# A fused attention and MLP kernel whose work is in one hand-held list: the first keys loaded one head at a time, and the list reordered

## The chip, the cores and the metric

The kernel runs on one core of a Trainium2 chip. A core has a matrix engine (TensorE, "PE"; its weight loads are shown apart as "PEld"), a vector engine (VectorE, "DVE"), an activation engine (ScalarE, "ACT"), a general engine (GpSimd, "POOL") and a queue engine (SyncE, "SP") that here only issues DMAs. Each engine runs its own instructions in program order and waits on semaphores for the others. Sixteen DMA engines serve all queues. The metric is the device time of one execution in microseconds (us), lower is better. A profiled execution gives a trace; its span is the time from the first to the last instruction, a little under the device time.

## What is computed

Causal attention over 4 batches, 8 heads, 768 tokens and 64 dimensions, then a two-layer MLP. Heads 0, 2 and 6 ("retrieval") see the whole past; the other five ("streaming") see the last 64 keys and the first 4.

```python
scores = scale * np.matmul(q, k.transpose(0, 1, 3, 2))
...
stream_keep = causal & (is_sink | in_win)
...
a = np.exp(scores)
a = a / (np.sum(a, axis=-1, keepdims=True) + 1e-09)
return np.matmul(a, v).astype(np.float32)
...
h = x @ w_in
g = np.maximum(h, 0.0) + alpha * np.minimum(h, 0.0)
return (g @ w_out).astype(np.float32)
```

x is the attention output with the heads side by side: 3,072 tokens of 512. w_in is 512 x 2048, w_out 2048 x 512, alpha one slope per hidden unit. All inputs are fp32 in DRAM; the kernel computes in bf16 and accumulates in fp32.

## The kernel before

**Pieces.** Two heads form a pair: (2,6), (1,5), (0,4), (3,7), four pairs in each batch, sixteen in all, numbered n = 0 to 15. A pair is a full 128 partitions: head hh = 0 in the lower 64, hh = 1 in the upper 64. The MLP works on token groups t = 0 to 7, two to a batch: 512 tokens (t even) and 256 (t odd).

**Items.** Every step is a named item, a small function that emits the instructions of one step:

- `Lq`n, `Lk`n, `Lv`n load a pair's fp32 queries, keys and values (lines 203 to 247), nearly all through SP's queue. For pair 0 the queries are two items, Lq0.0 and Lq0.1, and the keys one, Lk0, whose first head goes through ACT's queue and the second through SP's. `La` loads the slopes through ACT's queue. `wi`0 to 7 and `wo`0 to 3 load w_in and w_out in pieces through POOL's queue, with a cast. P items 0 to 3 need wi0 and wi1, 4 to 7 wi2 and wi3, 8 to 11 wi4 and wi5, 12 to 15 wi6 and wi7; the u-th quarter of an O item needs wo(u).
- `Cq`, `Ck`, `Cv` cast them to bf16, on POOL, ACT or DVE by a table (for n = 1 to 5 on POOL; Cq6 and Cq7 on ACT; later ones on DVE). `Tq`, `Tk` transpose on PE, `tq`, `tk` copy the result out of PSUM (tk on DVE for n under 4, on ACT for 4 to 7). From pair 8 on, `Dq` and `Dk` transpose by DMA from SP's queue instead.
- `S`n.hh.m is a part of the scores (PE), `s` its exponential (ACT), `m` its mask (DVE, from pair 4 on; before that the mask is added by PE, lines 462 and 501). `A`n.hh multiplies by the values (PE), `a` divides (DVE), `X`n transposes the pair's output into xT: by PE with the copy `x` for pairs 0 to 3 and 15, else by DMA from SP.
- `P`t.f is the first MLP layer for a block of 128 hidden units (two blocks for t odd); its three parts P0.f.0 to P0.f.2 take the pairs as they come. `p` is the negative half (ACT), `g` joins the halves (DVE). `O`t.s.u is a quarter of the second layer for 128 tokens, `o` copies it out of PSUM (ACT) and sends it to DRAM (POOL's queue for t under 6, else SP's). The last 128 tokens are done in three column cuts, `L0` to `L2` with `l0` to `l2`.
- `warm`0 to 8 are matmuls on zeros whose result nobody reads (32, 3, 14, and six times 4): they keep PE busy while it waits for the first loads. The rest (`kz`, `vz`, `sz`, `nms`, `nmr`, `id`, `near`, ...) fills constants and masks. A few items, such as m8.0.2, emit nothing.

**The order.** ORDER, a list of 1,076 names, is walked once; each engine and each DMA queue gets its instructions in that order. The list is the schedule: there is no other. The batches overlap by it: while the MLP of one batch runs on PE, the attention of the next one is woven in. Below, "pass one" is the stretch in which batch 0's MLP runs beside pairs 4 to 7, "pass two" batch 1's MLP beside pairs 8 to 11, "pass three" batch 2's beside 12 to 15.

**Bursts.** From pair 4 on, scores listed near each other are gathered and emitted as one burst. An item that can't stand beside them, such as a P, O or A item, ends the gathering. If each head of the burst has at least 576 columns, the two heads' matmuls are interleaved, each on half of PE's rows (line 430); if not, they run one by one on all rows, with zeros in the other half of the keys (line 423).

**PSUM.** Eight banks of PSUM are handed out by `take` (the one given back longest ago among the choices) and given back by `give`, both at the time of emission; the banks of the three cuts are not given back.

Of the kernel before, what the change touches and what calls it, by code (L numbers as in the profile page):

```python
# [14 lines left out]
busy zero La id warm0 kz3 Lq0.0 sz1 vz2 nms nmr so1 vz0 Lq0.1 Lk1 warm8 warm5 warm3 kz1 qz0 one Lq1 Lk0 Ck0.0 Cq0.0  # L15
Tq0.0 tq0.0 Tk0.0 qz kz0 kz2 idf warm2 Lk2 tk0.0 Ck1.0 Ck1.1 Cq0.1 Tk1 S0.0.1 s0.0.1 Tq0.1 S0.0.0 Cq1 warm7 Lv0 tk1.0
sz2 vz1 vz3 Tq1 Lq2 Ck0.1 S0.0.2 s0.0.0 tk1.1 Tk0.1 Ck2.1 tq1 S1.1.0 s0.0.2 Ck2.0 warm4 tq0.1 nz0 s1.1.0 Cq2 tk0.1 Cv0
Lk3 S0.1.0 kfz0 Lv1 vo ro0 Ck3.1 s0.1.0 Lq3 Ck3.0 wi1 wi0 Cq3 sz0 S1.0.0 so2 Al s1.0.0 so0 al S0.1.1 s0.1.1 Lv2 Tq2
Tk2 tk2.1 tk2.0 S0.1.2 S1.0.1 A0.0 s0.1.2 a0.0 Cv1 A0.1 a0.1 Cv2 s1.0.1 tq2 S1.1.1 nz1 Tk3 S2.0.1 tk3.0 s1.1.1 S2.0.2
X0 s2.0.1 x0 wi6 s2.0.2 wi7 Lv3 Lq5 Tq3 tk3.1 S2.0.0 wi5 m4.0.2 warm6 S2.1.0 A1.0 a1.0 Lk4 s2.0.0 A2.0 S2.1.1 A1.1  # L20
a2.0 tq3 s2.1.0 a1.1 S3.0.0 s2.1.1 s3.0.0 A2.1 a2.1 S3.1.1 X1 S3.0.1 s3.0.1 Lk5 wi4 kfz2 Cv3.0 Cq5 Lk7 wi2 X2 Ck4.0
s3.1.1 S3.1.0 x1 P0.0.0 x2 P0.0.1 A3.0 P0.1.0 P0.1.1 Lk6 Lq4 Lq6 Ck4.1 kfz3 nr Cv3.1 s3.1.0 A3.1 Lv7 Lv5 Lq7 Ck5.0 wi3
a3.0 P0.2.0 Tq5 tq5 P0.3.0 P0.3.1 a3.1 X3 x3 ns kfz1 P0.2.1 Tk4 near2 P1.2 P0.1.2 P0.2.2 P0.0.2 p1.2 p0.1 g0.1 Ck5.1
P1.0 P0.3.2 g1.2 P0.15 tk4.0 p0.2 g0.2 p0.15 wo0 p1.0 Lk8 near0 g0.15 g1.0 ro1 P1.12 P1.14 m12.1.2 p0.0 g0.0 wo1 tk4.1
p1.12 P0.14 g1.12 p0.14 g0.14 P0.13 p0.13 g0.13 P0.11 p1.14 Tk5 Ck7.1 g1.14 P1.10 tk5.0 p0.11 p1.10 Ck6.0 Ck7.0 g0.11
m8.0.2 tk5.1 wo2 Lv6 Lv4 P0.10 P0.8 p0.8 Tk7 g1.10 wo3 Cq4 Lk9 P0.12 P1.8 p0.10 g0.8 p0.12 g0.10 Tq4 P0.6 P0.9 p0.3
# [24 lines left out]
O2.1.2 O3.1.1 O3.1.2 X10 o2.2 O3.1.3 O2.1.3 X11 P4.11 o2.1 P4.14 P5.14 p5.14 P4.4 P4.6 Lk12 P5.0 g5.14 Ck12 p4.4 p4.6
p4.11 P4.13 g4.6 p4.14 g4.11 Lq14 g4.14 P5.12 P4.5 P4.12 p4.13 Dq12 o3.1 p5.0 g4.13 Cq14 g5.0 Dk13.1 p4.5 g4.5 g4.4
Cv14 P4.9 p4.9 g4.9 P4.2 P5.2 Dq13 p5.12 g5.12 P4.10 p5.2 P4.8 P4.1 p4.12 g4.12 g5.2 p4.10 g4.10 Lv15 Dk12.0 Dk12.1
Lv12 p4.1 Lk14 Lv13 Lk15 g4.1 P4.7 P4.0 p4.2 g4.2 p4.8 g4.8 p4.0 p4.7 g4.7 P4.15 Cv12 S13.0.1 s13.0.1 S12.0.5 S12.0.3
P4.3 P5.4 g4.0 s12.0.3 p4.3 s12.0.5 S12.1.5 S12.0.1 S12.0.0 S13.1.1 s13.1.1 Dq14 g4.3 Cq15 Ck14 m12.0.3 O4.3.0 s12.1.5
s12.0.1 O4.3.1 O4.3.2 s12.0.0 p4.15 g4.15 P5.6 P5.10 S12.1.1 S12.0.4 S12.0.2 p5.4 S13.1.0 g5.4 p5.6 s12.0.4 Dk14.0
P5.8 s13.1.0 s12.0.2 p5.8 s12.1.1 m12.0.0 g5.6 O4.3.3 Ck15 p5.10 g5.8 m12.0.1 g5.10 m12.0.4 O5.1.0 Cv13 O5.1.1 O5.1.2
o4.3 Dk14.1 S14.1.1 S14.0.0 S12.1.4 S14.0.1 S14.1.0 S13.0.2 m12.1.1 s14.1.0 s13.0.2 O4.2.0 m12.0.5 A12.0 s14.0.1
s12.1.4 O5.1.3 Dk15.1 s14.1.1 Dk15.0 s14.0.0 a12.0 m14.0.1 Dq15 o5.1 O4.2.1 S13.1.2 S12.1.2 S14.1.2 S14.0.4 m13.1.0
m14.0.0 m13.0.1 S14.0.5 S13.0.0 O4.2.2 O4.2.3 s13.1.2 m13.1.2 m13.1.1 s13.0.0 s14.0.4 s14.0.5 m13.0.2 S12.1.0 m12.1.5  # L60
s14.1.2 S12.1.3 S15.0.0 S14.0.3 m13.0.0 A13.1 o4.2 s12.1.0 s12.1.2 A13.0 s15.0.0 O5.0.0 s12.1.3 s14.0.3 m14.0.4 Cv15
a13.1 O5.0.1 a13.0 S15.0.1 S15.0.2 m12.1.0 S15.1.0 S15.1.2 S15.1.1 S14.0.2 O4.1.0 s15.0.2 s15.1.0 m12.1.4 s14.0.2
s15.1.1 m14.1.1 m14.0.5 m14.1.2 m12.1.3 m14.1.0 A12.1 m14.0.3 A14.1 A14.0 a14.0 s15.1.2 a14.1 m15.0.2 s15.0.1 a12.1
O4.1.1 X13 O4.0.0 O4.0.1 O4.0.2 O4.0.3 m15.0.0 m15.1.1 O4.1.2 m15.0.1 m15.1.2 m15.1.0 A15.0 o4.0 A15.1 a15.0 O4.1.3
a15.1 O5.0.2 X15 O5.0.3 X14 x15 o4.1 o5.0 X12 P6.11 p6.11 P6.2 P6.15 P6.10 p6.10 P7.4 P6.0 P6.1 g6.11 g6.10 p6.1 P6.6
P7.8 p6.15 g6.15 g6.1 p6.0 g6.0 P6.5 p7.4 p6.5 p6.6 g7.4 g6.6 g6.5 P6.3 P6.12 P7.2 p6.3 p6.12 g6.12 p6.2 g6.2 P6.4
p7.8 P7.6 P6.14 g6.3 g7.8 p7.6 p6.4 g7.6 g6.4 P7.10 P6.7 P6.8 p6.8 p6.7 P7.0 P6.9 P6.13 g6.7 p7.2 g7.2 g6.8 p7.10
g7.10 p6.9 P7.14 O6.3.0 P7.12 p6.13 g6.13 p7.12 O6.0.0 O6.0.1 O6.1.0 p7.0 g7.0 g6.9 O6.3.1 O7.0.0 O6.3.2 O6.1.1 p7.14
p6.14 g6.14 g7.12 O6.3.3 o6.3 O6.0.2 O6.1.2 O6.1.3 o6.1 O6.0.3 o6.0 O6.2.0 O6.2.1 O6.2.2 O7.0.1 O7.0.2 O6.2.3 o6.2
m12.0.2 g7.14 L2 l2 O7.0.3 o7.0 L0 L1 l1 warm1 l0  # L70
""".split()


@with_exitstack
def kernel(
    ctx: ExitStack,
    tc: tile.TileContext,
    q: bass.AP,
    k: bass.AP,
    v: bass.AP,  # L80
    is_retrieval: bass.AP,
# [114 lines left out]
    def heads(n):  # L196
        return PAIRS[n % 4]
# [5 lines left out]
    def load_q(n, eng=nc.sync):  # L203
# [643 lines left out]
```

## Time and profile before

| | us |
|---|---|
| median of 3 runs | 229.27 |
| the three runs | 229.27, 229.27, 230.81 |
| profiled execution, device time | 229.83 |
| its span | 228.0 |

| work, by the page's costliest groups | count | busy us |
|---|---|---|
| first MLP layer, PE, line 597 | 512 | 86.5 |
| second MLP layer, PE, line 617 | 368 | 85.4 |
| scores from pair 4 on, packed, PE, line 430 | 181 | 11.7 |
| scores, other, PE, lines 413 and 423 (413 alone in the group) | 68 | 11.3 |
| attention times values, PE, line 552 | 536 | 11.0 + 10.1 |
| `g`, DVE, line 609 | 128 | 71.0 |
| `p`, ACT, line 602 | 96 | 54.4 |
| exponentials, ACT, lines 469 and 517 | 63 + 45 | 37.1 + 21.0 |

How to read it: "busy" is the time in which at least one instruction of the group is running. PE's matmuls overlap in the pipeline, so a matmul's own duration is longer than its cost, and a busy PE may still be waiting for short moments; the distance from one matmul's start to the next one's is the better measure. The "list work" of the prediction adds up such distances. In rows of the timeline, the text in brackets is the engine's idle time before the instruction and what ended it.

### The profile page before, as it was taken

How to read it: one execution, taken by the hardware profiler on the slowest of the kernel's cores; microseconds unless marked ns; L12 is line 12 of the kernel's file. 1: busy time of each engine (PE TensorE's matmuls, PEld its weight loads, DVE VectorE, ACT ScalarE, POOL GpSimd, SP SyncE). 2: the span in 40 equal slices, each digit the busy share in tenths (PEclk: the TensorE clock that was granted, in tenths of full speed). 3: DMA queues.
4: the chain of work that ended last, by engine and by line, in shares of the span. 5: the costliest groups of instructions: out<-in, count | busy, mean ns of one | idle time of the engine just before them, and what ended most of it. 6: DMA issues, size and time to landing. Idle time of an engine off the chain costs nothing.

```text
span 228.0 us, 5239 instructions
## 1 busy us (share of the span) xinstructions
PE 222.4 (98%) x2005; PEld 135.9 (60%) x2005; DVE 151.6 (66%) x395; ACT 139.6 (61%) x284; POOL 45.8 (20%) x91
## 2 busy tenths in 40 slices
PE   8999999999999999999999999999999999999994
PEld 8789876563455656555556455556556555664454
DVE  7769849966389816899699219987586535966000
ACT  2689559999799128477994136787594236563311
POOL 6769996101130001000400001000110110000000
PEclk9999999999999999999999999999999999999999
DMA  6999999999998798989969899995821420000213
GB/s 190 313 229 210 286 223 262 206 197 241 206 287 142 132 204 227 172 192 181 254 153 199 194 266 146 218 166 107 132 93 38 116 95 0 0 4 0 88 66 123
DMA packets 95417, 37.39 MB, mean 164 GB/s; under 512 B 82440, under 2 KB 93600, under 8 KB 95392
## 3 DMA queue, kind: packets, MB, share of 16 engines
q1 hardware_dynamic: 89136, 27.73, 61.2%
q0 software_dynamic: 5792, 8.93, 17.1%
q10 hardware_dynamic: 464, 0.40, 0.5%
q8 instruction: 15, 0.25, 0.5%
q14 instruction: 10, 0.08, 0.2%
HBM read 27.71 MB, written 6.29 MB: 149 GB/s over the span
## 4 chain that ended last, share of the span: by engine, by line
PE 92%; ACT 3%; DVE 2%; issue 1%; DVEq 0%; ACTq 0%
PE P L597 35%; PE P L617 34%; PE P L552 7%; PE P L430 4%; PE P L687 3%; PE P L413 2%; PE P L363 2%; PE P L636 2%; ACT neg L602 1%; PE P L501 1%; DVE kT L392 1%; PE P L423 1%; PE P L577 1%; ACT kT L392 1%; ACT eS L523 1%
## 5 line engine op out<-in xcount | busy, mean ns | idle before, releaser
L609 DVE SCALAR_TENSOR_TENSOR g<-neg,oma,P 128x256 bf16<-128x256 f32 (+1 forms) x128 | 71.0, 608 | 35.9 <-ACT neg L602 35.5
L597 PE MATMUL P<-xT,w_in_b 128*128 128x512 bf16 (+1 forms) x512 | 86.5, 326 | 0.0
L617 PE MATMUL P<-w_out_b,g 128*128 128x512 bf16 x368 | 85.4, 379 | 0.0
L602 ACT ACTIVATE neg<-P 128x512 f32<-128x512 f32 x96 | 54.4, 600 | 27.2 <-PE P L597 22.6
L597 PEld LDWEIGHTS <-w_in_b 128*128 128x128 bf16 x512 | 49.5, 98 | 31.7 <-DVE g L609 0.2
L617 PEld LDWEIGHTS <-g 128*128 128x128 bf16 x368 | 33.8, 98 | 37.2 <-issue 1.2
L469 ACT ACTIVATE eR<-P 128x448 bf16<-128x448 f32 (+4 forms) x63 | 37.1, 636 | 5.4 <-PE P L430 2.3
L623 ACT COPY ot<-P 128x512 f32<-128x512 f32 x23 | 13.8, 602 | 37.8 <-PE P L617 32.9
L627 POOL DMA_DIRECT2D out_dram<-ot x18 | 10.3, 571 | 113.2 <-ACT ot L623 113.0
L517 ACT ACTIVATE eS<-P 128x352 bf16<-128x352 f32 x45 | 21.0, 493 | 3.7 <-PE P L430 3.7
L563 DVE TENSOR_TENSOR xn<-P,rcp 128x448 bf16<-128x448 f32 (+1 forms) x32 | 19.5, 608 | 1.1
L528 DVE TENSOR_TENSOR eS<-eS,ms_near 128x352 bf16<-128x352 bf16 x45 | 14.3, 334 | 4.4 <-ACT eS L517 4.2
L479 DVE TENSOR_TENSOR eR<-eR,mr_near 128x128 bf16<-128x128 bf16 (+5 forms) x54 | 12.1, 252 | 4.0 <-ACT eR L469 4.0
L430 PE MATMUL P<-qT,kT 64*128 64x176 bf16 (+13 forms) x181 | 11.7, 251 | 0.3 <-DVE g L609 0.3
L430 PEld LDWEIGHTS <-kT 64*128 64x128 bf16 x181 | 7.2, 94 | 7.6 <-issue 6.8
L413 PE MATMUL P<-qT,kT 128*128 128x192 bf16 (+14 forms) x68 | 11.3, 251 | 0.3 <-ACT eS L523 0.3
L552 PE MATMUL P<-vb,eS 128*128 128x65 bf16 x260 | 11.0, 193 | 0.4 <-DVE eS L528 0.4
L552 PEld LDWEIGHTS <-eS 128*128 128x128 bf16 x260 | 9.7, 97 | 2.9 <-DVE eS L528 0.6
L562 DVE RECIPROCAL rcp<-P 128x7 f32<-128x7 f32 (+1 forms) x32 | 6.3, 198 | 7.1 <-PE P L552 6.9
L552 PE MATMUL P<-vb,eR 128*128 128x65 bf16 x276 | 10.1, 192 | 0.0
L552 PEld LDWEIGHTS <-eR 128*128 128x128 bf16 x276 | 9.4, 97 | 1.2
L645 DVE COPY ot<-P 128x128 f32<-128x128 f32 x1 | 0.3, 292 | 14.3 <-PE P L636 14.3
(95 smaller groups left out, 175.5 us busy)
## 6 DMA issues: line engine op xcount, KB each, us to landing
out_dram<-ot POOLq DMA_DIRECT2D x18, 256.0 KB, 3.6
kf<-in_k_dram SPq DMA_DIRECT2D x21, 192.0 KB
qf<-in_q_dram SPq DMA_DIRECT2D x18, 192.0 KB
vf<-in_v_dram SPq DMA_DIRECT2D x14, 196.0 KB
qf<-in_q_dram SPq DMA_DIRECT2D x7, 384.0 KB
vf<-in_v_dram SPq DMA_DIRECT2D x12, 192.0 KB
w_in_b<-in_moe_w_in_dram POOLq DMA_DIRECT2D x8, 256.0 KB, 9.7
w_out_b<-in_moe_w_out_dram POOLq DMA_DIRECT2D x4, 512.0 KB, 13.4
```

The costliest lines, as they stand in the source:

```text
L413: nc.tensor.matmul(to, keys, queries, start=True, stop=stop)
L430: nc.tensor.matmul(to, keys[own], queries[own], start=True, stop=True)
L469: nc.scalar.activation(ebuf[n, hh][:, lo:hi].rearrange("p (x c) -> p x c", x=len(parts)), P[:, got[0]:got[0] + len(parts), 0:(hi - lo) // ...
L517: nc.scalar.activation(slots, sc[:, 0:352].rearrange("p (s c) -> p s c", c=176), AF.Exp, scale=scale)
L528: nc.vector.tensor_tensor(slots, slots, ms_near[:, 0:2, :] if m == 0 else ms_near[:, 1:3, :], op=ALU.mult)
L552: nc.tensor.matmul(pav[:, i, :], e[:, o:o + 128], vv[:, j, hh, 0:D + 1], start=(m == 0), stop=(m == len(terms) - 1))
L563: nc.vector.tensor_tensor(xn[n][:, 0:nt, D * hh:D * hh + D], pav[:, :, 0:D], rcp.to_broadcast([128, nt, D]), op=ALU.mult)
L597: nc.tensor.matmul(psg[:, w * i:w * (i + 1)], w_in_b[:, c, 128 * fb:128 * (fb + 1)], xT[:, c, o:o + w], start=(x == 0), stop=(x == 3))
L602: nc.scalar.activation(neg[t, f], bank(held["P", t, f][0]), AF.Relu, scale=-1.0)
L609: nc.vector.scalar_tensor_tensor(g_buf[t % 2][:, fb, 0:w], neg[t, f][:, c], oma[:, fb:fb + 1], bank(got[0])[:, c], op0=ALU.mult, op1=ALU.add)
L617: nc.tensor.matmul(bank(held["O", t, s][0]), g_buf[t % 2][:, f, 128 * s:128 * (s + 1)], w_out_b[:, f, :], start=(f == 0), stop=(f == 15))
L623: nc.scalar.copy(ot, bank(got[0]))
```

## The change

1. `load_k` can load one head of a pair. Pair 0's keys become two items, Lk0.0 (through ACT's queue) and Lk0.1 (through SP's), in place of Lk0. The DMAs themselves are the same.
2. `P2_cut_out` gives its PSUM bank back.
3. ORDER is replaced by another order of the same items (1,077 names).

```diff
-    def load_k(n):
+    def load_k(n, of=range(2)):
         if n >= CROSS:
             load_rows(n, k, kf)
             return
-        for hh, h in enumerate(heads(n)):
+        for hh in of:
+            h = heads(n)[hh]
             T = row_tokens(n, h)
...
         (nc.scalar, nc.sync)[x % 2].dma_start(out[r:r + 128, lo:hi], last[0][:, lo:hi])
+        give(got)
...
         item(f"Cq0.{i}", cast_q0, i)
+        item(f"Lk0.{i}", load_k, 0, [i])
...
-        item(f"Lk{n}", load_k, n)
+            item(f"Lk{n}", load_k, n)
```

Of the two lists, the stretches that the prediction speaks of. The head:

```diff
-busy zero La id warm0 kz3 Lq0.0 sz1 vz2 nms nmr so1 vz0 Lq0.1 Lk1 warm8 warm5 warm3 kz1 qz0 one Lq1 Lk0 Ck0.0 Cq0.0
-Tq0.0 tq0.0 Tk0.0 qz kz0 kz2 idf warm2 Lk2 tk0.0 Ck1.0 Ck1.1 Cq0.1 Tk1 S0.0.1 s0.0.1 Tq0.1 S0.0.0 Cq1 warm7 Lv0 tk1.0
...
+kz3 busy vz1 warm0 warm7 zero nmr sz1 qz0 Lk0.0 Ck0.0 kz1 m8.0.2 kz0 nms Lq0.0 id Tk0.0 Cq0.0 Tq0.0 kz2 tk0.0 Lk1
+warm2 ro0 La Ck1.0 Ck1.1 Tk1 tk1.0 tq0.0 S0.0.0 warm6 Lq1 Cq1 sz2 s0.0.0 Lq0.1 warm5 vz3 tk1.1 Tq1 S0.0.2 Lk0.1 tq1
...
+A2.0 wi7 s2.1.1 s2.1.0 Cq5 S3.1.1 a2.0 s3.1.1 A2.1 a2.1 S3.0.0 s3.0.0 S3.0.1 wi6 X1 x1 Tq5 X2 x2 S3.1.0 P0.2.0 Lv3
```

The part of pass one around w_out, new list:

```diff
+g0.13 P1.8 S5.0.1 p0.4 g0.4 Lq9 P1.6 Cv4 p1.6 g1.6 s5.0.1 m5.0.1 m5.1.1 Ck6.1 S4.0.2 P0.11 s4.0.2 p0.11 g0.11 p0.5
+g0.5 P0.7 p0.7 g0.7 Tq6 tq6 near0 p1.8 S5.0.0 P0.9 m5.1.2 s5.0.0 m5.0.0 m5.0.2 Ck7.0 m4.1.2 O0.3.0 p0.9 Tk6 tk6.1 Cq7
+Ck7.1 O0.1.0 wo1 O0.1.1 tk6.0 O0.2.0 Tk7 m5.1.0 g0.9 Tq7 tq7 tk7.0 S4.0.5 wo2 Cv7 Cq8 tk7.1 g1.8 O0.2.1 m4.0.1 O0.2.2
+wo3 O0.2.3 O0.1.2 O0.1.3 S4.0.4 o0.2 S4.0.0 S6.1.0 Lv6 S4.1.4 S7.0.0 s4.0.5 S4.1.0 s4.1.0 Cv5 O0.3.1 m4.0.3 o0.1
...
+m7.1.2 S7.0.2 S6.0.0 s4.1.3 m4.1.3 m7.0.0 m6.0.3 s6.0.4 m6.0.4 m6.0.5 S6.1.2 X5 A7.1 s4.1.2 Cv6 s4.1.5 m4.1.5 s6.0.0
+O1.1.3 s7.0.2 S6.0.1 m7.0.2 A4.1 A7.0 s6.1.2 s6.0.1 m6.1.2 m6.0.0 m6.0.1 s6.0.2 Lv9 a4.1 A6.1 a6.1 A6.0 a6.0 X4 X6
```

POOL's casts and weight loads in their order, before and after, with the constants between them left out:

```
before: Ck1.0 Ck1.1 Cq0.1 Cq1 Ck0.1 Ck2.1 Ck2.0 Cq2 Cv0 Ck3.1 Ck3.0 wi1 wi0 Cq3 Cv1 Cv2 wi6 wi7 wi5 wi4 Cv3.0 Cq5 wi2 Ck4.0
        Ck4.1 Ck5.0 wi3 Ck5.1 wo0 wo1 wo2 wo3 Cq4 Cv5 Cv4
after:  Ck1.0 Ck1.1 Cq1 Cq0.1 Ck0.1 Ck2.0 wi1 Ck2.1 Cv0 Cq2 Ck3.0 Cq3 Ck3.1 wi0 Cv1 Cv2 wi7 Cq5 wi6 Cv3.0 Ck4.0 wi5 wi4 Ck4.1
        wi2 Cq4 Ck5.0 wi3 Ck5.1 wo0 Cv4 wo1 wo2 wo3 Cv5
```

SP's loads up to pair 7 (and 8 and 9 where they come between):

```
before: q0.0 q0.1 k1 q1 k0.1 k2 v0 q2 k3 v1 q3 v2 v3 q5 k4 k5 k7 k6 q4 q6 v7 v5 q7 k8 v6 v4
after:  q0.0 k1 q1 q0.1 k0.1 v0 k2 q2 k3 q3 v1 v2 q5 v3 k4 q4 k5 k6 v4 q6 v7 q7 k7 q8 v5 q9 v6
```

The last scores of pair 12 ahead of A12.0 in pass three (the old list has A12.0 some lines further on):

```diff
-s12.0.1 O4.3.1 O4.3.2 s12.0.0 p4.15 g4.15 P5.6 P5.10 S12.1.1 S12.0.4 S12.0.2 p5.4 S13.1.0 g5.4 p5.6 s12.0.4 Dk14.0
...
+s12.1.1 g4.0 Cv12 P4.15 p4.12 g4.7 P4.6 S13.0.1 p4.6 s13.0.1 m12.1.2 g4.6 p4.8 P5.4 g4.8 p5.4 P5.14 O4.3.0 O4.3.1
+O5.1.0 g4.12 p4.15 S13.1.0 S13.1.1 S12.1.5 g5.4 p5.14 S13.0.2 g4.15 S12.0.4 s13.0.2 Lv13 Cv13 g5.14 m13.0.2 s13.1.0
+O4.3.2 m13.1.0 O4.3.3 Dk15.1 Dk14.1 s12.0.4 m12.0.4 A12.0 s13.1.1 Dk14.0 S14.0.1 s12.1.5 S14.0.4 S14.1.0 S12.1.4 o4.3
```

## The prediction

> **What bounds the kernel now.** I read the busy line first, then busy time by stretch, then single rows of the timeline.
>
> ```profile
> PE 222.4 (98%) x2005; PEld 135.9 (60%) x2005; DVE 151.6 (66%) x395; ACT 139.6 (61%) x284; POOL 45.8 (20%) x91
> ...
> 0.00:27.00 27.00, 25.11 (x382) 22.87 (x383) 21.31 (x60) 17.94 (x25) 20.92 (x44) 1.00 1.02 247
> 27.00:76.00 49.00, 48.24 (x472) 28.94 (x471) 36.37 (x101) 40.82 (x90) 14.77 (x31) 1.00 1.11 219
> 76.00:130.00 54.00, 54.00 (x455) 30.36 (x452) 40.04 (x107) 31.51 (x69) 5.35 (x9) 1.00 0.99 189
> 130.00:183.00 53.00, 53.00 (x446) 29.85 (x445) 36.08 (x96) 31.46 (x69) 4.22 (x7) 1.00 0.75 144
> ```
>
> The columns of a stretch are its length, then busy time of PE, PEld, DVE, ACT and POOL, the granted clock, the DMA share and GB/s. From 76 to 183 us PE is never idle: no order can gain there except by making PE's own work shorter. What an order can win lies before 76 us: 1.89 us idle in the first 27, 0.76 in the next 49, and waits too short to empty PE's pipeline. The DMA engines are full there (share 1.02 and 1.11), and ACT, 40.8 of 49 us busy, is nearly a second bound.
>
> To cost PE work I took the distance from one matmul's start to the next of its kind: 216 ns at 512 columns, 109 at 256, 56 at 128, 29 at 65. "List work" below is PE's sum by these up to a point of the order list; trace time minus list work is what PE has lost by then. In before, list work up to P1.2 is 25.21 us and P1.2 starts at 31.05: 5.84 lost. Up to P2.9 it is 74.48 against 82.41: 7.93 lost. So pass one lost 2.09 between them.
>
> **The bursts of scores.** Counting by the rule in emit_burst, the old list makes 26 bursts, of which 17 have at least 576 columns in each head and run as two half arrays side by side. The new list makes 41, with 13 such. Two rows price them:
>
> ```profile
> 57.11 0.55 PE L430 MATMUL P<-qT,kT 64*128 64x176 bf16 x9
> ...
> 101.50 0.55 PE L423 MATMUL P<-qT,kT 128*128 128x448 bf16 x4
> ```
>
> The first is a packed burst of 896 and 800 columns: the next matmul starts at 57.59, so it costs 0.48 us, which is 896 columns at 2.4 per ns (0.37) and 0.11 over; the matmul ahead of a packed burst also lasts 0.10 longer. The second is two unpacked bursts, 896 columns: the next starts at 101.89, 0.39, nothing over. Old: 4,424 columns alone (1.84) + 20,088 columns of the longer heads (8.37) + 17 x 0.216 = 13.89. New: 12,208 (5.09) + 15,744 (6.56) + 13 x 0.216 = 14.45. **+0.57**: 0.18, 0.26 and 0.13 in passes one to three. Nothing hides this.
> The Trainium skill (TensorEngine Tiling, Theoretical Speedup) promises up to twice the speed for a contraction of 64, which speaks against unpacking; by it alone, with no price for switching, the term would be 11.65 - 10.21 = +1.43. The same page (Key Properties) says that a change of mode drains the array, and the 0.216 us of these rows agrees.
>
> **The head.** Old: the slopes' DMA goes ahead of the keys on ACT's queue, 0.45 us of issue.
>
> ```profile
> 0.81 0.42 ACTq L288 DMA_DIRECT2D alpha_r<-in_moe_alpha_dram  x1
> 1.26 0.44 ACTq L223 DMA_DIRECT2D kf<-in_k_dram  x1
> ...
> 5.41 0.51 ACT L328 CAST g<-kf 128x384 bf16<-128x384 f32 x1 [2.40 <-DMA kf<-in_k_dram]
> ```
>
> The cast of k0.0 waits until 5.41; the first q, issued at 0.82, was used at 3.39. New: k0.0 is first on ACT and only q0.0 goes beside it, q0.1 having moved behind the second pair's keys and queries. I put its landing at q's 3.39 plus one load (0.68, from nine loads between 3.39 and 9.51): 4.1, cast done 4.6. Bounds: 3.4 and 5.0 (only La's 0.45 saved). Warm-ups ahead fall from 44 to 36, so PE comes to Tk0.0 at 1.07 + 36 x 0.107 = 4.9. In the old trace starts 107 ns apart last until 6.2 us and 56 ns after, so Tk0.0 and Tq0.0, twelve transposes, would take 1.3 us at the slow pace, to 6.2; ACT's copy (0.79) ends at 7.1, and the first score starts there instead of 7.91. Gain 0.8. All loads keep their number; La, now behind ACT's first cast, has until Al, some five microseconds after it; what stands behind it on ACT loses 0.4 us of issue, inside ACT's wait for Tq0.0.
> The Trainium skill (TensorE: Matmul & The Clock Gate, Part 1) puts the switch at about 3.4 us of activity in a free-running window; by that PE would be fast from about 4.5 us and the head would gain 0.6 more. The row (5.1 us after the first matmul) decides.
>
> Then a load takes over. Tq5, at 29.1 us before, moves ahead of X2. Its cast waited in before until q5 landed at 26.0. Six loads landed between q2 (13.5) and q5, 2.08 us each; in the new queue q5 is one load earlier: 23.9, cast (0.82) done 24.8, Tq5 at 24.9. PE would come to it at list work 19.80 + 5.84 - 0.80 - 0.38 (X2 had waited 0.38 for a2.1; 1.74 us now lie between them instead of 1.13) = 24.5. So PE waits 0.4 and has lost 5.10 from there on: **-0.74** (0 to -1.14).
>
> **Pass one after that.** Old losses of 2.09: a burst behind ACT (0.46), A5.1 behind its mask (0.66), Tk7, O0.1.0 (0.16, 0.20), small change. The new list takes pair 5's scores some 10 us earlier, so A5.1 has 16.7 us of PE work behind its last score instead of 6.2: those go. Two waits are new.
> First, w_out. GpSimd issues all its DMAs in program order, and Cv4 now stands ahead of wo1, wo2, wo3:
>
> ```profile
> 34.80 3.01 POOL L696 DMA_DIRECT2D w_out_b<-in_moe_w_out_dram  x4
> 40.58 0.83 POOL L315 CAST natq<-qf 128x768 bf16<-128x768 f32 x1 [2.77 <-DMA qf<-in_q_dram]
> 56.37 0.93 POOL L348 CAST vb<-vf 128x896 bf16<-128x896 f32 x1 [14.97 <-DMA vf<-in_v_dram]
> ```
>
> Old: four issues from 34.80, landing (by the trace's semaphores) at 44.3, 47.7, 51.0 and 54.4, before any cast that waits. New: v4 has the place in SP's queue that q4 had, which landed at 40.5 (second row); but it has 1,536 packets of 256 bytes, q4 256 large ones. From 27 to 51 us the packet records show SP's and GpSimd's queues moving equally many, about 148 per us each, against some 550 per us for SP alone. Ahead of and with v4 after 27.5 us are 3,300 packets: 14 us beside the remaining weights take 2,100, the rest 2.2: v4 at 43.9. So Cv4 ends at 41.4 to 44.9, wo1 goes out there, lands some 8 us later (the first w_in chunk took 6.5 and is half the size), the others 3.35 apart: wo3 at 56.3 to 59.7. O0.2.3 needs it at list work 52.14 + 5.1 = 57.2. Wait 0 to 2.5; I take 1.2, the middle, for want of a nearer row.
> Second, the last exponentials: after the last packed burst six run on ACT (0.54 + 0.61 + 0.66 + 0.62 + 0.57 + 0.58 = 3.58) before A6.0, and PE has 2.37 of work (one O quarter, one burst, A4.1, A7.0, A6.1). Wait 0 to 1.2; I take 0.6, since before, ACT and PE came to A6.0 together. So 1.8 instead of 2.09: **-0.29**.
>
> **Passes two and three.** Most distances from a score to its A are longer (A9.0 9.5 us of PE work instead of 2.5), which gains nothing where PE never waited. A12.0 is shorter: 1.72 instead of 5.97, for three exponentials (1.60) and a mask (0.22): **+0.3** with handovers, 0 to 1. X7 and Dq9 have seven us of PE work ahead of their readers and cost nothing; without that cover a DMA transpose is 1.25 us of SP. The tail, L0 and L1, is the same; L2 earlier and the bank given back move nothing.
>
> **Sum** against the profiled execution (span 228.0, time 229.83): +0.18 - 0.74 - 0.29 + 0.39 + 0.3 = -0.16. The median of the three runs is 229.27; the same difference gives **229.1**.
>
> **Rivals.**
> No change, as summed (own range 227.6 to 230.8): 0.45.
> Faster: v4 lands at 41 and ACT keeps ahead, so neither new wait appears: -1.8 more, 227.3, and 226.9 with the whole head. For it: ACT is 4 us of work further at O0.1.0. Against: ACT had to do 39.8 us of work between 32.1 and 74.9 and was idle only 3.0. 0.20.
> Slower, by w_out: if the weights hold SP's queue back further, v4 lands at 45 to 48 and wo3 at 61 to 64: waits of 4 to 7 at O0.2.2 and O0.2.3 in place of 1.2, of which ACT's lead recovers one: about 232. It decides from v4 landing later than 42.4. For it: Cv5 waited 14.97 us on just such a load. 0.22.
> The change does not do at the end what it does at the start: loads, not keys, set the head (Cq2 waited 2.21 on q2), the gain of 0.74 is gone, 229.8: 0.13.
> A measurement here tells about 1% (2.3 us) from no change. Below 227.0: half the faster case and a little, 0.12. Above 231.6: three quarters of the slower case, a tenth of the first, a fifth of the last: 0.24. Between: 0.64. The range 226.9 to 232.2 leaves out the ends of the two outer cases.
>
> **What would show it.** 41 bursts, 13 of them on L430's half arrays, 0.57 us more; the first score at 7.1; Tq5 started by q5's landing; Cv4 on POOL with a wait and w_out issued behind it, after 41 us; PE idle at O0.2.2 or O0.2.3 on w_out; none from 85 to 155. Wrong if PE waits in passes two and three, or if Cv4 finds v4 landed.

## The result, and the profile after

| | before | after |
|---|---|---|
| median, us | 229.34 (20 runs, 228.38 to 231.76) | 230.83 (20 runs, 229.62 to 233.72) |
| ratio | | 1.006, 95% interval 1.0038 to 1.0083 |
| profiled execution, us (span) | 229.83 (228.0) | 229.83 (228.1) |
| bursts, packed | 26, 17 | 41, 13 |
| list work, us | 215.93 | 216.50 |

The change makes the kernel slower by about 1.4 us. Ratios here and below leave disturbed runs out, medians of one kernel's runs do not. The two profiled executions took equally long, but they do not stand alike in their groups: 229.83 is above the median of before's runs and the third fastest of after's. So a comparison of these two traces alone would show no loss, and profiles of the same list taken again have to be read beside it.

The busy line of the page and busy time by stretch, after:

```profile
PE 222.3 (97%) x2005; PEld 137.3 (60%) x2005; DVE 150.1 (66%) x395; ACT 139.6 (61%) x284; POOL 45.5 (20%) x91
```

```profile
0.00:27.00 27.00, 24.76 (x387) 22.40 (x388) 21.06 (x60) 18.06 (x24) 18.25 (x41) 1.00 1.05 236
27.00:76.00 49.00, 48.23 (x475) 29.85 (x473) 35.74 (x104) 40.49 (x90) 17.50 (x33) 1.00 1.14 233
76.00:130.00 54.00, 54.00 (x444) 30.62 (x443) 39.70 (x105) 30.41 (x67) 4.35 (x7) 1.00 1.12 190
130.00:183.00 53.00, 53.00 (x445) 30.45 (x444) 35.31 (x95) 32.10 (x70) 4.32 (x8) 1.00 0.65 137
```

PE still has no idle time from 76 to 183 us, so what the order wins or loses lies before; only the dearer bursts count after it. The chain of waits, which follows the end back to its causes, has changed (first what before's page says of it, then after's, then the longest of after's pieces up to 60 us: start, length, what):

```profile
PE 92%; ACT 3%; DVE 2%; issue 1%; DVEq 0%; ACTq 0%
```

```profile
PE 73%; DMA 21%; POOL 2%; DVE 1%; SPq 1%; issue 1%; POOLq 0%
```

```profile
1.74 4.49 DMA kf<-in_k_dram
7.39 0.93 DVE kT L393
8.85 0.94 DVE kT L393
10.34 8.94 DMA vf<-in_v_dram
19.40 0.94 POOL vb L349
20.70 6.76 DMA kf<-in_k_dram
28.70 13.63 DMA vf<-in_v_dram
42.45 0.93 POOL vb L349
44.82 14.38 DMA w_out_b<-in_moe_w_out_dram
59.24 2.75 PE P L618 x12
```

In before the chain is PE with small pieces of ACT and DVE. In after it runs through loads up to 59.24: v1 and its cast, k4, v4 and its cast (Cv4), and the last piece of w_out, which GpSimd may issue only behind Cv4. PE's own rows show it at those places (start, length, and in brackets the idle time and what ended it):

```profile
20.39 0.22 PE L553 MATMUL P<-vb,eS 128*128 128x65 bf16 x2 [0.37 <-POOL vb L349]
20.79 0.88 PE L553 MATMUL P<-vb,eS 128*128 128x65 bf16 x24 [0.18 <-POOL vb L307]
...
33.08 1.89 PE L598 MATMUL P<-xT,w_in_b 128*128 128x512 bf16 x8 [0.68 <-DMA w_in_b<-in_moe_w_in_dram]
```

The first two are A1.0, behind v1's cast and its sink rows; the third is P0.12, behind wi6. Below, "lost" is again trace time minus list work at an item. Three profiles of the new list, e1 and e16 being repeats, stand beside two of the old (e5 is a repeat):

| | before | e5 | after | e1 | e16 |
|---|---|---|---|---|---|
| time of the profiled run | 229.83 | 229.46 | 229.83 | 230.45 | 231.60 |
| lost at A0.0 | 5.12 | 5.23 | 4.30 | 4.23 | 4.30 |
| at P1 (first P item of t = 1) | 5.84 | 5.96 | 5.73 | 6.39 | 7.28 |
| at O0.2.3 | 6.86 | 7.22 | 7.11 | 7.61 | 8.71 |
| at P2 | 7.77 | 7.52 | 7.38 | 7.89 | 8.98 |
| at L1 | 8.98 | 8.73 | 8.60 | 9.10 | 10.20 |

From 229.83 to 230.45 to 231.60 the time grows by 0.62 and 1.15, and what is lost by P2 by 0.51 and 1.09; from P2 to L1 it grows by 1.22, 1.21 and 1.22, the same each time. So the new list's slower runs are slower before P2. At the new list's median that is, by estimate, some 0.7 us more lost by P2 than in the old list (between e1's 7.89 and e16's 8.98 by time, 8.3, against 7.5 to 7.8), with 0.57 of list work beside it: 1.3 of the 1.5 between the medians.

### The profile page after: what moved, and what is told of

It reads as the page before. It is cut to its first block, busy times and chain, and to the rows that moved or that the text cites. A ratio compares the mean times of both kernels' runs of the same rounds, so it can differ in the third digit from the quotient of the medians.

```text
span 228.1 us, 5239 instructions
## 1 busy us (share of the span) xinstructions
PE 222.3 (97%) x2005; PEld 137.3 (60%) x2005; DVE 150.1 (66%) x395; ACT 139.6 (61%) x284; POOL 45.5 (20%) x91
## 4 chain that ended last, share of the span: by engine, by line
PE 73%; DMA 21%; POOL 2%; DVE 1%; SPq 1%; issue 1%; POOLq 0%
PE P L618 33%; PE P L598 27%; DMA vf<-in_v_dram 10%; DMA w_out_b<-in_moe_w_out_dram 6%; PE P L553 6%; DMA kf<-in_k_dram 5%; PE P L431 3%; PE P L637 2%; PE P L424 2%; POOL vb L349 1%; DVE kT L393 1%; POOL w_out_b L698 0%; SPq L247 0%; PE P L364 0%; POOL g L329 0%
## 5 line engine op out<-in xcount | busy, mean ns | idle before, releaser
L610 DVE SCALAR_TENSOR_TENSOR g<-neg,oma,P 128x512 bf16<-128x512 f32 (+1 forms) x128 | 71.6, 608 | 36.0 <-ACT neg L603 35.5
L598 PE MATMUL P<-xT,w_in_b 128*128 128x256 bf16 (+1 forms) x512 | 88.4, 326 | 0.7 <-DMA w_in_b<-in_moe_w_in_dram 0.7
L518 ACT ACTIVATE eS<-P 128x352 bf16<-128x352 f32 x45 | 20.5, 481 | 4.8 <-PE P L431 3.3
L480 DVE TENSOR_TENSOR eR<-eR,mr_near 128x128 bf16<-128x128 bf16 (+5 forms) x54 | 10.5, 226 | 6.7 <-ACT eR L470 6.5
L414 PE MATMUL P<-qT,kT 128*128 128x192 bf16 (+13 forms) x68 | 11.1, 251 | 0.1
L424 PE MATMUL P<-qT,kT 128*128 128x176 bf16 (+10 forms) x60 | 9.2, 251 | 0.0
L431 PE MATMUL P<-qT,kT 64*128 64x176 bf16 (+12 forms) x144 | 9.0, 251 | 0.0
L431 PEld LDWEIGHTS <-kT 64*128 64x128 bf16 x144 | 5.9, 94 | 4.8 <-issue 4.0
```

Source lines behind the costliest of these rows:

```text
L424: nc.tensor.matmul(*x[3:6], start=True, stop=True)
L431: nc.tensor.matmul(to, keys[own], queries[own], start=True, stop=True)
L518: nc.scalar.activation(slots, sc[:, 0:352].rearrange("p (s c) -> p s c", c=176), AF.Exp, scale=scale)
L598: nc.tensor.matmul(psg[:, w * i:w * (i + 1)], w_in_b[:, c, 128 * fb:128 * (fb + 1)], xT[:, c, o:o + w], start=(x == 0), stop=(x == 3))
L610: nc.vector.scalar_tensor_tensor(g_buf[t % 2][:, fb, 0:w], neg[t, f][:, c], oma[:, fb:fb + 1], bank(got[0])[:, c], op0=ALU.mult, op1=ALU.add)
```

## The experiments

Every kernel stood beside runs of before on its own chip; five batches, with medians of before of 229.34 (e1 to e4), 229.28 (e5 to e8), 229.51 (e9 to e12), 229.54 (e13 to e15) and 229.53 (e16 to e18). "Old list" means the new kernel's code with the old order, keys split, the two names side by side; only e5 has the old code too.

**The two lists again (e1, e5).** No edit: e1 is after itself, e5 is before itself, with its old code.

> The new list unchanged, for a second profile and more times. Theory A (the new list's head and pass one are paced by DMA landings: v1 at A1.0, wi6 at P0.12, wo3 at O0.2.3): the median stays 1 to 2 us over the old list's, and a run slower than the first profile's 228.1 us span shows its extra time as longer waits at these three places, up to 1 us each, and none after 76 us. Theory B (passes two and three are slower than their list work says): the extra time lies after 76 us.

> The old kernel unchanged, for a second profile. Theory A (list work plus DMA-paced waits): list work 215.93 us as in the first profile, PE's lost time at the end between 8.5 and 9.2 us, no wait on a load or a weight over 0.3 us on PE; ratio 1.000.

e1: 230.44, ratio 1.0049 (1.0024 to 1.0074). e5: 229.04, 1.0001 (0.9989 to 1.0013). So both kernels repeat themselves. That the loss is the order's, and not that of the split keys or of the bank given back, is shown by e11 below: the new code with the old order but for one item, at 1.0005. e5's twelve runs lie within 228.78 to 229.50, e1's within 229.00 to 231.59.

**List work alone (e8, e13).** Order of the old list, another packing bound.

```diff
-    SPLIT = 576
+    SPLIT = 100000     # e8
+    SPLIT = 1000       # e13
```

> The old list with the bound for packing raised so that no burst is packed: the scores from pair 4 on take 42,192 columns, 17.58 us of list work instead of 13.89, so +3.69. Theory A (no PE idle after 76 us, so list work passes on in full): +3 to +3.9 us, ratio 1.013 to 1.017; in passes two and three alone +2.4. Theory that unpacked bursts are hidden behind ACT and DMA: under +1.5 us.

> The old list with the packing bound at 1000 columns instead of 576: 9 packed bursts instead of 17, list work 216.92 (0.51, 0.11 and 0.36 more in passes one to three), the order untouched. Theory A (list work passes on after 76 us in full and in pass one in part, and nothing else happens): 0.47 to 1.0 above before, median 229.8 to 230.5, ratio 1.002 to 1.0045, lost at L1 8.4 to 9.0. Rival (any shift of PE against the loads also widens the spread of the runs): ratio 1.006 or more, more than a third of the runs over 231.

e8, with no burst packed (list work +3.69): 233.23, 1.0189 (1.0157 to 1.0222); PE ends 2.9 to 3.1 us later than in the two old profiles, and 0.6 to 0.8 less is lost by L1. Of this 0.3 to 0.5 is there at P1 already, ahead of the first burst, and is that run's own; from P1 to P2 another 0.3 to 0.7 less is lost. From P2 to L1 it takes 2.74 us more than the two old profiles, where list work says 2.52. e13 (+0.99, of which 0.51 in pass one): 230.04 against 229.54, 1.0017 (0.9993 to 1.0041), its runs within 229.51 to 230.94; 1.002 or more was expected. So unpacking costs what the rows say after 76 us, or a little more; in pass one PE's waits absorb part of it. The new list's 0.57 is worth 0.4 to 0.57, and dearer bursts alone do not spread the runs.

**Which part of the order (e2, e3, e12, e18, e14, e15).** Splices: up to an item the one order, then the items not yet named in the other order.

```diff
-... a7.0 a7.1 X7 P2.3 Ck8 P2.8 Ck9 Dk9.0 ...     (new list at X7)
+... a7.0 a7.1 X7 m4.0.2 m12.1.2 m14.0.2 m8.1.2 Ck8 m10.0.2 P2.9 P2.3 p2.9 ...     (e2: new, then old)
-... X4 X6 a7.1 a7.0 X7 P2.9 P2.3 p2.9 ...     (old list at X7)
+... a7.1 a7.0 X7 m6.0.2 Cq8 Cq9 Lv9 P2.3 P2.8 Ck9 ...     (e3, e12: old, then new)
+... Tk4 tq5 x3 nz0 nz1 m4.0.2 Lk5 Lk7 wi2 Lk6 Lq4 Lq6 ...     (e18: new up to x3, then old)
```

> New list up to X7 (head and pass one), then what is left in the old list's order: 32 bursts, 15 packed, 14.06 us of bursts instead of 14.45. Theory A: 0.39 us better than the whole new list and still about 1 us (0.4%) over the old one; PE never idle after 76 us. Theory B: within 0.3 us of the old list plus 0.18 for pass one's bursts, 229.5 us.

> Old list up to X7 (head and pass one), then what is left in the new list's order: 35 bursts, 15 packed, 14.28 us of bursts. Theory A: the old list plus 0.39 us for the bursts of passes two and three, 229.7 us, ratio 1.002. Theory B: most of the 1.5 us, 230.4 us or more, with PE waiting after 76 us.

> The old list up to X7, then the rest in the new order, a second time (35 bursts, 15 packed, list work 216.32, 0.39 more than before). Its first measurement was 1.0058 where 1.002 was expected. Theory A (the new order's rest brings SP's and GpSimd's items of pass two into pass one at other places, so that loads of pass one come later): 1.004 to 1.008 again, with lost time at A6.0 or O0 0.5 us or more over before's and a wait on a load there. Rival (the first measurement was high by chance, only list work counts): 1.001 to 1.003, lost at L1 as in before, 8.6 to 9.0.

> The new list up to x3 (the head, about 26 us), then the old order: 26 bursts, 17 packed, list work 215.93 as in before. Theory A (the new head gains 0.8 us at A0.0 and gives it back to late loads before P1, and its late w_in adds a wait of 0.5 to 0.9 at the first whole P item): lost at A0.0 4.2 to 4.6, at P1 5.7 to 6.4; median 0.3 to 1.2 us above before, ratio 1.001 to 1.005. Rival (the new head is good by itself and is spoilt by pass one's order): lost at P1 5.0 to 5.5, ratio 0.996 to 0.999.

| | list work | median | ratio (95%) |
|---|---|---|---|
| e2: new up to X7, old behind | +0.18 | 231.20 | 1.0051 (1.0016 to 1.0086) |
| e18: new up to x3 (some 26 us), old behind | 0 | 231.27 | 1.0066 (1.0033 to 1.0099) |
| e3: old up to X7, new behind | +0.39 | 231.11 | 1.0058 (1.0029 to 1.0087) |
| e12: the same again | +0.39 | 230.70 | 1.0064 (1.0041 to 1.0087) |

e18 is the clearest: the new head alone, with not one burst changed, costs as much as the whole change. e2 was to be 0.39 us better than the whole new list and is not. And the old list up to X7 with the new one behind it (e3, e12) costs as much again: the parts do not add up to the whole, and why is open. e18's rows of PE:

```profile
21.11 0.22 PE L553 MATMUL P<-vb,eS 128*128 128x65 bf16 x2 [0.79 <-POOL vb L349]
21.51 0.88 PE L553 MATMUL P<-vb,eS 128*128 128x65 bf16 x24 [0.18 <-POOL vb L307]
...
39.90 1.02 PE L598 MATMUL P<-xT,w_in_b 128*128 128x512 bf16 x4 [1.00 <-ACT neg L603]
```

A1.0 waits for v1's cast as in after, and lost goes from 4.67 at A0.0 to 5.95 at A1.0 and 6.45 at P1: the expected range at P1 is just passed, that of the median (0.3 to 1.2 us) by half a microsecond. The third row is P0.11, which needs wi4. The bracket names ACT, but by the trace's DMA records wi4 landed at 39.81, 0.09 before the start: the wait was for the weight, and 1.16 us of lost time appear there.

e3 and e12 missed Theory A's first expectation (1.002) twice, and the reason is open. Up to X7 their list is before's. e12's profile, 230.04, the fastest of its six runs, has lost 7.56 at P2 and 8.98 at L1 against before's 7.77 and 8.98, and PE ends 0.39 later, which is the list work. e3's profile is of its slowest run, 232.78. Both have one wait behind X7 that neither before nor after has, ahead of the first burst of pass two, 0.20 us of lost time in e12 and 0.43 in e3:

```profile
90.42 0.31 PE L424 MATMUL P<-qT,kT 128*128 128x176 bf16 x2 [0.27 <-DMA qT<-natq]
```

It goes with the splice: the new order has Lv9 ahead of X7, the old one behind it, so SP issues v9's four loads, 1.9 us, ahead of the transposes of k9 and q9. e14 and e15 were to find the pass.

```diff
-X10 o2.2 O3.1.3 O2.1.3 X11 P4.11 o2.1 P4.14 ...     (old list at X11)
+X10 o2.2 O3.1.3 O2.1.3 X11 ...     (e14: from here the new order)
```

> The old list up to X11, then the new order (pass three and the tail): 16 packed bursts, list work 216.05, 0.12 more than before. Theory A (only list work counts): ratio 0.999 to 1.002. Rival (the new order behind X7 costs 1.2 us, and it lies in pass three, where A12.0 follows closely on its last score): ratio 1.004 or more, with a wait on ACT or DVE after 140 us.

> The old list up to X7, the new order up to X11, the old one again from there: 16 packed bursts, list work 216.19, 0.26 more than before. Theory A (only list work counts): ratio 1.000 to 1.003. Rival (the new order behind X7 costs 1.2 us, and it lies in pass two, whose first loads and DMA transposes stand at other places of SP's queue and run beside the end of pass one): ratio 1.004 or more, with a wait of PE between 76 and 110 us or more lost by P2 than before.

e14: 231.35, 1.0065 (1.0034 to 1.0096), with this row of PE:

```profile
139.18 0.54 PE L424 MATMUL P<-qT,kT 128*128 128x448 bf16 x4 [1.63 <-DMA qT<-natq]
```

It is a product of the splice: the old order loads k12 in pass three, the new one in pass two, and the splice loads it late and needs it early. Neither after nor e12 has that wait, so e14 tells nothing of the new pass three. e15: 231.01, 1.0034 (1.0003 to 1.0065), 0.26 of list work, 0.2 more lost from P2 to P4 than in before, at the same burst as in e3 and e12 (0.25). So of the loss behind X7 beyond list work that the ratios show, about 1 us in e3 and e12, the profiles show 0.2 to 0.4, as a product of the splice; the rest stays open.

**w_out (e4, e6).** New list; wo1 to wo3 go out right behind wo0, ahead of Cv4; in e6 k7 and q6 are also issued earlier.

```diff
-P1.10 wo0 P0.1.2 ns
+P1.10 wo0 wo1 wo2 wo3 P0.1.2 ns
-P0.2.2 p0.2 Lk6 g0.3 g0.2
+P0.2.2 p0.2 Lk6 Lk7 Lq6 g0.3 g0.2     # e6 only
```

> The new list with wo1, wo2, wo3 right behind wo0, so ahead of the masks and of Cv4 on POOL's queue; nothing else moved. Theory A: w_out is issued at 38 to 41 us instead of 43 to 46 and wo3 lands by 56; the wait of 0.26 us at O0.2.3 goes in the profile, and the median falls by 0.3 to 1 us, since that wait is longer in slower runs. v4 and v5 land a little later beside the weights, which costs nothing unless A5.1 starts to wait. Theory B: no change within 0.2 us.

> The kernel with w_out ahead of Cv4, and besides it Lk7 and Lq6 moved right behind Lk6 on SP's queue, as the old list has them. Theory A (the DMA queues share the engines by packets, so a transfer moved forward makes the one behind it late): the 2.1 us wait of Tk7 on k7's cast goes, no wait on w_out comes back, and the time falls from 232.8 to 230 or below, ratio 1.003 or less. Rival (w_out's traffic at 38 to 57 us costs whatever stands behind it, always about 2 us): another wait of 1 us or more turns up in pass one and the time stays over 231.5 us.

e4: 232.82, 1.0168 (1.0129 to 1.0206), slower where a gain was expected. The wait on w_out is gone (pieces landed from 46.0 to 57.1), but k7 shares the DMA engines with them; its cast on DVE and then Tk7 wait:

```profile
56.85 0.36 DVE L329 CAST natm<-kf 128x384 bf16<-128x384 f32 x1 [2.10 <-DMA kf<-in_k_dram]
```

```profile
58.13 0.51 PE L364 MATMUL P<-ident,natm 128*128 128x128 bf16 x6 [1.93 <-DVE natm L329]
```

e6: 234.78, 1.0246 (1.0217 to 1.0275): now wi5 and wi4 come late (P1.10 waits 1.36), then q7 (Tq7 1.56). Those waits are from a run of 232.94; the four slowest of its six, 234.67 and more, show a mean clock of 0.993 besides, the other two of 0.998 and more. In pass one a load moved forward only chooses which other one is late.

**The early half of w_in (e7, e9, e16, e17, e10).** In the new list wi1 is issued by GpSimd at 11.23 us, in the old one at 16.21. e9 makes that one move in the old list; e7, and e17 beside the unchanged e16, undo it in the new one; e10 is e7 up to X7 with the old order behind.

```diff
-Ck2.1 tq1 S1.1.0 ... Lq3 Ck3.0 wi1 wi0 Cq3     (e9, in the old list)
+Ck2.1 wi1 tq1 S1.1.0 ... Lq3 Ck3.0 wi0 Cq3
-tq0.1 tk0.1 wi1 S1.1.0 ... s2.0.1 Ck3.1 wi0 a0.1     (e7, e17, in the new list)
+tq0.1 tk0.1 S1.1.0 ... s2.0.1 Ck3.1 wi1 wi0 a0.1
```

> The new list with one item moved: wi1, issued by POOL at 11.2 us, goes next to wi0 at about 17.6. Theory A: v1 no longer shares the engines with it and lands a microsecond earlier, so A1.0 and Tk3 wait 0.5 to 1 us less; but wi7 and wi6 follow later by as much, so P0.12 waits more and PE has lost the same at O0 (6.8 to 7.4 us): within 0.5 us of the new list. Rival (the early weights are a plain mistake in the list): the gain stays and the time falls by 0.8 us or more.

> One item moved in the old list: wi1, from just ahead of wi0 on GpSimd's queue (four casts later) to right behind Ck2.1, where the new list has it (about 6 us earlier). Nothing else differs from before; list work 215.93. Theory A (an early w_in half takes its share of the DMA engines from the keys, queries and values that PE waits for in the first 30 us): wi1 issued at about 11 to 12 us instead of 17; k3, q3 and v1 land later by 0.3 to 1 us; lost time at P1 up by 0.3 to 1.2 us; median 229.7 to 230.5, ratio 1.002 to 1.005. Rival (the loads of the old head have slack for it, the harm in the new list came from v1 standing behind q3): lost at P1 as in before (5.8 to 6.0), ratio 0.999 to 1.001.

> The new list up to X7 with wi1 moved to just ahead of wi0, then the rest in the old order: 32 bursts, 15 packed, list work 216.11, so 0.39 less than the new list after 76 us. Theory A (the new list's loss is 0.57 of list work plus the early wi1): 1 to 1.5 us below the new list and 0.4 below the one with wi1 late alone: median 228.7 to 229.3, ratio 0.997 to 1.001, no wait of PE after 85 us. Rival (the two orders do not fit together at X7, or pass one's loads vary too much for 0.4 us to be seen): ratio 1.003 or more, with a wait on a load in pass one.

> The new list unchanged, third time, beside e17 on one chip. Both theories: ratio 1.003 to 1.008, list work 216.50, lost at P1 5.7 to 6.5, a wait on w_in at the first P items of pass one.

> The new list with wi1 just ahead of wi0 on GpSimd's queue, beside e16 on one chip. Theory A (the early w_in half costs about 1 us in the new list, as it cost 3.6 in the old): median 0.8 to 1.5 us below e16's, ratio 0.999 to 1.003. Rival (e7's low median was its quiet chip; v3 and k4 come late instead of v1 and k3): median within 0.5 us of e16's, ratio 1.003 to 1.007.

| | median | ratio (95%) |
|---|---|---|
| e9: old list, wi1 early | 233.08 | 1.0170 (1.0151 to 1.0189) |
| e7: new list, wi1 late | 229.33 | 1.0026 (0.9997 to 1.0055) |
| e16: new list | 231.21 | 1.0065 (1.0035 to 1.0095) |
| e17: new list, wi1 late, same chip as e16 | 230.00 | 1.0038 (1.0004 to 1.0072) |
| e10: e7 up to X7, old behind | 230.83 | 1.0051 (1.0022 to 1.0081) |

One DMA of 256 KB, moved by itself to about where the new list has it, costs 3.6 us in the old list, three times what was expected. GpSimd's rows, e9:

```profile
10.30 0.77 POOL L694 DMA_DIRECT2D w_in_b<-in_moe_w_in_dram  x1
...
15.90 0.63 POOL L694 DMA_DIRECT2D w_in_b<-in_moe_w_in_dram  x1
20.54 0.83 POOL L316 CAST g<-qf 128x768 bf16<-128x768 f32 x1 [4.01 <-DMA qf<-in_q_dram]
21.30 0.94 POOL L349 CAST vb<-vf 128x896 bf16<-128x896 f32 x1
...
23.82 0.93 POOL L349 CAST vb<-vf 128x896 bf16<-128x896 f32 x1 [0.88 <-DMA vf<-in_v_dram]
...
25.94 0.61 POOL L694 DMA_DIRECT2D w_in_b<-in_moe_w_in_dram  x1
```

While wi1 and wi0 move, q3 comes late: its cast starts at 20.54, after a wait of 4.01 (in before at 17.60, without one). The cast blocks GpSimd, and everything behind it there goes out later: v1's cast (21.30; in before 18.36) and the third piece of w_in (25.94; in before 22.08). Lost goes from 5.05 at A0.0 to 8.08 at A1.0 and 10.94 at P1. Not all of that is waiting. The profiled run, 234.05, is the slowest of e9's five, and its PE had a lower clock behind the wait (the first row is Tq3, the second the first 27 us, where the clock is the third number from the end):

```profile
21.42 0.51 PE L364 MATMUL P<-ident,g 128*128 128x128 bf16 x6 [2.03 <-POOL g L316]
```

```profile
0.00:27.00 27.00, 23.06 (x328) 20.87 (x329) 18.05 (x53) 16.16 (x21) 17.60 (x37) 0.94 0.99 233
```

The granted clock is 0.50 from 22.3 to 25.8 us, so some 1.7 us of the 10.94 (an estimate, half of that stretch) are the clock's. The other four runs, 232.96 to 233.87, show a mean clock of 1.000, and the median is one of theirs. So moving a weight forward made the weights late. The new list has the same on a smaller scale. Landing of the eight pieces of w_in, in their order, from the trace's DMA records (us):

```
before  22.7  25.0  30.3  32.0  33.8  35.9  37.8  40.2
after   18.8  22.8  29.4  32.9  35.2  37.1  39.1  41.4
e16     18.5  23.3  30.0  33.6  38.3  39.8  41.2  43.2
e18     19.6  23.6  29.4  34.3  37.6  39.8  42.4  44.0
e17     23.3  24.7  30.1  31.9  33.7  35.7  37.8  41.3
e9      17.6  23.0  33.4  35.1  37.0  39.5  41.7  43.4
```

With wi1 early the first piece comes 3 to 5 us sooner, when nobody needs it yet, and from the fourth on they come 0.9 to 4.6 later (e17 apart). The casts that cause it can be seen in e16:

```profile
24.70 0.82 POOL L316 CAST natq<-qf 128x768 bf16<-128x768 f32 x1 [1.14 <-DMA qf<-in_q_dram]
25.46 0.61 POOL L694 DMA_DIRECT2D w_in_b<-in_moe_w_in_dram  x1
29.91 0.50 POOL L329 CAST natm<-kf 128x384 bf16<-128x384 f32 x1 [2.87 <-DMA kf<-in_k_dram]
30.36 1.22 POOL L694 DMA_DIRECT2D w_in_b<-in_moe_w_in_dram  x2
```

and what PE makes of them (Tk4 behind k4's cast, then P1.10 behind wi4):

```profile
32.15 0.51 PE L364 MATMUL P<-ident,natm 128*128 128x128 bf16 x6 [1.25 <-POOL natm L329]
...
39.91 1.25 PE L598 MATMUL P<-xT,w_in_b 128*128 128x256 bf16 x9 [0.73 <-DMA w_in_b<-in_moe_w_in_dram]
```

In e17 pieces one to seven land as in before, within 0.6 us; lost at P1 is 5.02 instead of 7.28; and its median is 1.2 us below e16's on the same chip and 0.47 above before's, which is about the list work. That is Theory A's expectation; but by the ratios the difference is 0.6 us, not 1.2, and the two intervals overlap. e7's median went its rival's way, below the new list's, but its profile (the second slowest of its twelve runs, 231.36) shows v3 and k4 late instead and has lost 7.74 at P1. e16 itself has lost 7.28 there, where 5.7 to 6.5 was expected. And e10, which should have been faster still, has a median of 230.83 with a profile of 229.38 and runs from 229.19 to 232.21. So by the medians a late wi1 won back 1.2 of 1.7 us beside e16 and nearly all in e7's batch, and little in e10; what it is worth in the new list is not clear of noise.

One place is clear. From A0.0 to A1.0 the seven profiles of the new head with wi1 early (after, e1, e2, e4, e6, e16, e18) lose 0.50 to 1.66 us, the three with wi1 late (e7, e10, e17) 0.15 to 0.21, and before 0.15. v1 stands behind q3 on SP's queue in all ten, so that place in the queue, which e9's rival blamed, does not cause the wait at A1.0; the early wi1 does.

**Keys first, alone (e11).**

```diff
-busy zero La id warm0 ... one Lq1 Lk0.0 Lk0.1 Ck0.0
+busy zero Lk0.0 La id warm0 ... one Lq1 Lk0.1 Ck0.0
```

> One item moved in the old list: Lk0.0 ahead of La on ACT's queue, the first half of the change by itself; list work 215.93. Theory A (the first score can come earlier, but other loads set the pace before P1): k0.0's cast done 0.3 to 0.5 earlier (old 5.9), the first score up to 0.5 earlier, lost at A0.0 down by 0.2 to 0.5, lost at P1 as in before within 0.2; ratio 0.998 to 1.001. Rival (the head's gain passes on): lost at P1 down by 0.4 to 0.5, median 228.7 to 229.0, ratio 0.997 to 0.9985.

229.37, 1.0005 (0.9974 to 1.0035); lost at A0.0 5.17, at P1 5.89. The key's cast started at 4.17 instead of 5.41, yet PE's first transposes start at 5.87 as in before:

```profile
3.71 2.23 PE L689 MATMUL P<-busy 128*128 128x128 bf16 x19
5.87 1.10 PE L362 MATMUL P<-ident,g 128*64 128x128 bf16 x12
```

The first row is the rest of the warm-ups, 44 ahead of the transposes in this list. They, not the key, keep PE until 5.87; the new list has 36 ahead, and its transposes start at 4.69. So the early key by itself gives nothing; the fewer warm-ups by themselves were not run.

No kernel was faster than before.

## Why the prediction was wrong

It said no change, 229.1; the kernel became 0.6% slower, 230.83 in the median. That is between two of the rivals, loads that set the head (229.8) and w_out (232); the mechanisms of both were seen, that of w_out at a smaller size.

- **Bursts, +0.57: right.** 41 bursts, 13 packed; from P2 to L1 after takes 142.02 us against 141.6. e8 and e13 price it on the chip. One limit: of the 0.18 in pass one PE's waits may absorb a part, so that 0.4 to 0.57 is left.
- **The head's gain at the first score: the number right, the path not.** It started at 7.19 (7.1 was said), k0.0's cast was done at 4.61 (4.6), and 0.82 is won at A0.0. But the transposes were not at the slow pace: in after PE's starts are 107 ns apart until 4.25 us and 56 ns from there on (until 6.2 in before, 5.4 in e1), so ACT's copy ended at 6.37 and not at 7.1. The first score then stood behind Tk1, which waited for the cast of k1:

```profile
6.84 0.51 PE L364 MATMUL P<-ident,g 128*128 128x128 bf16 x6 [0.41 <-POOL g L329]
```

  Two errors cancelled, and that is luck: already here a load decided. The Trainium skill (TensorE: Matmul & The Clock Gate, Part 1), weighed in this part, puts the fast clock at about 3.4 us of activity. It came 3.2 us behind the first matmul in after, near that figure, but 4.3 in e1 and 5.1 in before, whose row the prediction let decide.
- **That it lasts, -0.74: wrong; this is the step that failed.** "Then a load takes over. Tq5" named the wrong load. q5 did come at 23.8 as worked out, but A1.0 already waited on v1's cast, Tk3 on a cast of k3 behind q3's, and at P1 the gain was 0.11 in after, a loss of 0.55 in e1 and of 1.44 in e16. The cause of the wait at A1.0 is a move that the prediction listed and did not cost: wi1, five us earlier on GpSimd's queue (0.50 to 1.66 us lost ahead of A1.0 with it, 0.15 to 0.21 without). "All loads keep their number" is true and not enough, since they share the engines with it. e18 shows the head alone costing 1.7 us in the median and 1.5 by the ratio, e9 wi1 alone 3.6 in the old list; e17 has its return winning 1.2 in the median, 0.6 by the ratios. So the early wi1 took the gain away; how much of the 1.5 us it is, and what else varies from run to run between A1.0 and P1, is open. The rival "loads, not keys, set the head", given 0.13, was right about the direction and took only the gain away.
- **w_in: left out of the sum.** P0.12 (0.84), in other runs P1.4 (0.65), P1.10 (0.90), P0.11 (1.16), wait for w_in, because GpSimd's casts ahead of wi6, wi5 and wi4 wait for late loads. The queue's order was printed; only Cv4 ahead of w_out was costed by it.
- **w_out, 1.2: right place, the size in the wrong form.** Cv4 ended at 43.38 (41.4 to 44.9 was said), wo3 landed at 59.20 (56.3 to 59.7). PE's wait at O0.2.3 is only 0.26, since PE came there 1.8 us later than forecast. But it started 0.04 us behind wo3's landing in after, and also in e1, e16, e17, e2 and e10; only e7 of the seven came later than its weights. In those six O0.2.3 starts 16.8 to 17.1 us behind Cv4's start, wherever that is between 41.68 and 43.94. In before wo3 had landed 7.4 us ahead. So w_out is a second limit beside PE's other waits, and the time is not their sum: it is the later of the two. Taking the middle between the bounds hid this; forecast and truth at O0.2.3 are 6.3 lost against 7.11, 7.61 and 8.71. The rival said that it decides from v4 landing later than 42.4; v4 landed at 42.33, 42.83 and 43.82 in after, e1 and e16, so on both sides of that mark, and its 232 was too much.
- **Waits that go: right.** A5.1 no longer waits (0.66 in before; in e5 it did not wait either).
- **A6.0, 0.6, and A12.0, 0.3: too much.** Neither waited; PE came to A6.0 later than thought and ACT with its lead.
- **A misread row.** The 7.93 lost up to P2.9 in before is worked out from 82.41, where the last matmul of O0.0.3 ends; P2.9 starts at 82.24. So 7.77 was lost, and 1.93 in pass one instead of 2.09.
- **The Trainium skill on row tiling** (TensorEngine Tiling (Array Packing), Theoretical Speedup), by which alone unpacking would have cost 1.43: the measured 0.4 to 0.57 goes with the row that prices the switch.

For the profiled pair the sum came close, -0.16 against 0.00 in time, by luck. Of the head's gain 0.63 was missing and A12.0's 0.3 did not come. Pass one lost 1.65 (1.8 was said), but by other waits: 0.84 on w_in and 0.26 on w_out in place of 1.2 and 0.6. And the base misled: the pair compares a slower run of one kernel with a fast one of the other.

## What to carry to other kernels

Where the DMA engines are full, a transfer issued earlier takes its share from every load that is under way, and if casts that wait for those loads stand in the same in-order queue as later transfers, these go out later too: cost a moved DMA by all loads that land while it runs, not by its own issue. Two limits near each other are not added; find the later one, and look at what each has in hand (7.4 us in before, nothing in after). Before trusting one profile, see where its time stands among the runs of its kernel.

## What the runs showed of the hardware

One load of 256 KB through GpSimd's queue, issued six us earlier, held back a load of SP's queue so that its cast started 2.9 us later (e9, q3). The Trainium skill (DMA: Bandwidth & Descriptors, Issuing engines are not separate DMA queues) says that queues share the same engines; the row agrees. How far runs of one kernel differ goes with the order: on one chip the twelve runs of e5 lie within 0.72 us and before's own within 1.62 (but for one of 1,302 us), the twelve of e7 within 3.08. A wait of PE can be followed by a lower clock: in e9's trace PE was idle for 2.03 us up to 21.42, and the granted clock was 0.50 from 22.3 to 25.8; four other runs of the same kernel show a mean clock of 1.000. And a bracket can name the wrong engine: at P0.11 in e18 it says ACT, while the weight landed 0.09 us before.
